# SyncE's planned order kept in the program, and forty warm-up matmuls of other shapes, in an adaLN infini-attention block

## Chip, cores and metric

The kernel runs on one core of one Trainium2 chip. The metric is the device time of one execution in microseconds (us). Engines: PE is TensorE, ACT is ScalarE, DVE is VectorE, POOL is GpSimd, SP is SyncE, which here does nothing but issue DMA transfers.

## The reference

One transformer block over x of 2048 rows and 512 columns: a layer norm modulated by the condition c, causal attention in four segments with a compressive memory carried from segment to segment, a projection, and a feed-forward block with a squared ReLU.

```python
mod = (_silu(c) @ w_mod).reshape(c.shape[0], 6, 1, -1)
sa, ca, ga, sb, cb, gb = (mod[:, 0], mod[:, 1], ...)
h = _layernorm(x, axis=-1) * (1 + ca) + sa
x = x + ga * _A_ref(h, A_wq, A_wk, A_wv, A_wo, A_beta)
h = _layernorm(x, axis=-1) * (1 + cb) + sb
x = x + gb * _B_ref(h, B_w1, B_b1, B_w2, B_b2)
...
# _A_ref: 32 heads of 16, N = 4 segments of L = 512, phi(t) = elu(t) + 1
logits = jnp.einsum("bhqd,bhkd->bhqk", qs, ks) * scale + mask
a_dot = jnp.einsum("bhqk,bhkd->bhqd", _softmax(logits), vs)
o = g * (phi(qs) @ M) / (phi(qs) . z + 1e-6) + (1.0 - g) * a_dot
M = M + jnp.einsum("bhld,bhle->bhde", phi(ks), vs); z = z + phi(ks).sum()
...
# _B_ref: F = 1792
h = x @ w1 + b1
out = jnp.where(h > 0, h, 0) ** 2 @ w2 + b2
```

## The kernel before

**Stages.** The program first makes the modulation rows from c and w_mod (`bmod`, L541) and the normed and transposed rows of the first segment (tiles `lnf`, `HT`), and meanwhile loads the weights. Then come four segments of 512 rows. In each, the 32 heads go in four groups of eight, called units (u = 0 to 15 in all). A unit makes Q and K (`bqk`, L711 to L713) as a sum of three matmuls, since every operand is kept as a rounded half "hi" and a rest "lo". ACT casts the hi half of Q and K into the tile `sg` (L730), DVE subtracts to get the lo half (L732). Twelve small DMAs, the fills (function `fill`, L746 to L754), then rearrange `sg` in SBUF into the wide operand `ST`, from which the logits are formed (`ba`, L799; `bpb`, L956). Of the twelve, four read the hi halves of Q and K, four hi of Q and lo of K, four lo of Q and hi of K. `sg` has one buffer: the next unit's cast waits until the fills of this one have read it. For each quad of heads two more rows, `mt` (L867), go into ST by DMA. ACT makes the exponentials (`pt`), PE multiplies by V (`bpv`), and the outcome goes through DRAM (`o_dram` L1069, read back as `ot` L1117) to the projection with wo (`bwop`, L1101 to L1103). The feed-forward block goes last, over four segments and 14 blocks of F: `bh` (L1262 to L1264), bias `b1c` and ReLU on ACT, square on POOL, DVE or ACT, and `bpf` (L1290 to L1292). Its weights come as raw tiles `wr` (L1228, L1236) and are split in hi and lo (L1230, L1231).

**The order.** Every operation is a node of a planner, the class `Plan` (L226 to L370), with an engine, a duration and a priority. The table `ORDER` (L56 to L213) lists the nodes of each engine, SP among them, in the order in which they are to go; `run` (L1316) lays them out and takes the buffers of the pools, and `emit` writes them in that order. It does so inside `tc.manual_schedule(engines=...)` (L1317), which names the engines for which the order as written is kept. For an engine that isn't named, the framework's scheduler places the instructions itself. Before the change PE, DVE, ACT and POOL are named and SP isn't. On each engine instructions go in order: one that waits for a semaphore holds up all that stand behind it. Each DMA on SP also waits for the one issued eight before it, since eight semaphores go round. A fill, a load of x (L619) or of w_mod (L533) is one DMA; each takes some 0.4 to 0.7 us of SP's time to issue.

**The warm-ups.** PE has nothing to multiply while the first loads come, so 70 matmuls (L510 to L515) of the identity with itself, fp32 128x128, into a PSUM tile that nobody reads, stand in the gaps of the start: 49 ahead of the first `bmod`, 16 more up to the first `bqk`, five later, the last at some 80 us.

Of the kernel before, what the change touches and what calls it, by code (L numbers as in the profile page):

```python
# [9 lines left out]
F32R = mybir.dt.float32r  # L10
BF = mybir.dt.bfloat16
# [6 lines left out]
P = 128  # L18
# [4 lines left out]
F = 1792  # L23
# [202 lines left out]
class Plan:  # L226
# [17 lines left out]
    def op(self, eng, dur, fn, pr, after=(), mode=None, get=(), put=(), nb=0):  # L244
        n = Node()
        n.eng, n.dur, n.fn, n.pr, n.mode, n.get, n.put, n.nb = eng, dur, fn, pr, mode, tuple(get), tuple(put), nb
        n.lat = self.LAT[eng]
        n.outs, n.left, n.seq, n.at = [], 0, len(self.nodes), None
        for a in after:
            if a is not None:  # L250
                a.outs.append(n)
                n.left += 1
        for k in n.put:
            self.users[k] = self.users.get(k, 0) + 1
        self.nodes.append(n)
        return n
# [117 lines left out]
def block_kernel(ctx, tc, x, wq, wk, wv, wo, beta, w1, b1, w2, b2, c, wmod, out):  # L374
    nc = tc.nc
# [22 lines left out]
    ident = const.tile([P, P], F32, name="ident")  # L398
# [15 lines left out]
    sb = ph1.enter_context(tc.tile_pool(name="sb", bufs=1))  # L414
# [29 lines left out]
    PL = Plan(POOLS, ORDER)  # L444
# [3 lines left out]
    def bank(key):  # L448
        if key not in TL:
            TL[key] = ps.tile([P, 512], F32, name=f"b{key[0]}", tag=f"bank{PL.slot[key]}")  # L450
        return TL[key]
# [5 lines left out]
    def buf(pool, key, dt=F32):  # L457
        if key not in TL:
            home = xr_pool if pool == "xr" else sb
            TL[key] = home.tile(SHAPES[pool], dt, name=key[0], tag=f"{pool}{PL.slot[key]}")  # L460
        return TL[key]

    def pe(mode, dur, fn, pr, **kw):
        return op("PE", dur, fn, pr, mode=mode, **kw)

    def act(n, fn, pr, sbuf=False, sc=0, **kw):
        return op("ACT", n / 1200 + (0.095 if sbuf and n > 160 else 0.05) + 0.093 * sc, fn, pr, **kw)
# [4 lines left out]
    def sp(fn, pr, nb, n=1, **kw):  # L472
        return op("SP", 0.65 * n, fn, pr, nb=nb, **kw)
# [17 lines left out]
    def gates():  # L491
# [11 lines left out]
            get=[("#D", ("cs",))], put=["crow"])  # L503
# [4 lines left out]


    wk_ = ("warm",)  # L510
    for i in range(N_WARM):
        pe("F", 0.22, lambda: nc.tensor.matmul(bank(wk_)[:, :P], ident, ident, start=True, stop=True), 50.0,
           get=[("bank", wk_)] if i == 0 else (), put=[wk_], after=[n_w0] if i else ())
        if i == 0:
            n_w0 = PL.nodes[-1]  # L515

# [643 lines left out]
    for s in range(NS):  # L1160
# [6 lines left out]
        for cc in range(4):  # L1167
# [7 lines left out]
            for qd in (0, 1):  # L1175
                i = 2 * u + qd
                a_quad(u, qd, [i + k for k in K_A[qd]], i + K_T[qd])
            if s == 0 and cc == 1:
# [7 lines left out]
                n = pe("F", 0.9, lambda: nc.tensor.matmul(bank(b_), selc.to_broadcast([P, P]), TL[t_], start=True, stop=True),  # L1186
                       m0 + 3.1, after=[MODT[5]], get=[("#D", b_), ("oraw", tkey)], put=[t_])
                n = act(512, lambda: nc.scalar.copy(buf("oraw", tkey), bank(b_)), m0 + 3.11, after=[n], put=[b_])
                sp(lambda: nc.sync.dma_start(gb_dram, TL[tkey][0:1, :]), m0 + 3.12, 1 << 11, after=[n], put=[tkey])
            mem(u, [2 * u + k for k in K_MEM])  # L1190
            for qd in (0, 1):
                i = 2 * u + qd
# [52 lines left out]
    for t in range(4):  # L1245
        wo_tile(4 * NS - 4 + t, z - 2 + 0.3 * t)
    kb = ("b2b",)
    n = sp(lambda: nc.sync.dma_start(buf("xr", kb), bass.AP(tensor=b2.tensor, offset=b2.offset, ap=[[0, P], [1, D]])), z + 0.2, 1 << 18,
           get=[("xr", kb)], after=[X1N[4 * NS - 1]])
# [64 lines left out]
                last = s == NS - 1 and f >= NF - 2  # L1314
                ffn2(s, f, t, z + ST2 * (s * NF + (NF - 1 if last else f) + LAG) + (0.02 * t + 0.001 * f if last else 0.001 * t), RR[s, f])
    PL.run()  # L1316
    with tc.manual_schedule(engines={mybir.EngineType.PE, mybir.EngineType.DVE, mybir.EngineType.Activation, mybir.EngineType.Pool}):  # L1317
        PL.emit()


# [21 lines left out]
```

## Time and profile before

| | before |
|---|---|
| runs | 806.57, 807.46, 807.86 us, median 807.46 |
| span of the profiled execution | 804.3 us |
| PE busy | 792.1 us (98%) |
| DVE, ACT, POOL busy | 537.3, 440.5, 232.9 us |
| DMA moved | 65.23 MB in 51300 packets |
| fills (ST from sg) | 192 of 128 KB |

The profiled execution has no time of its own beside the span; the runs' median is 3.2 us above it. A timeline's row gives start and duration in us, engine (SPq is SyncE's queue of DMA issues), line, operation, tiles out and in, shape, the number of records, and in brackets the engine's idle time before it with what ended it. PE writes two records for one such fp32 matmul of the warm-up.

### The profile page before, as it was taken

To read this page: it belongs to the slowest core of one execution; us is meant where nothing else is said; L and a number is where in the kernel's file an instruction comes from. 1 tells how busy PE (TensorE), PEld (TensorE's weight loads), DVE (VectorE), ACT (ScalarE), POOL (GpSimd) and SP (SyncE) were. 2 spreads that over 40 slices of the span, in tenths; PEclk is the share of its full clock that TensorE was granted. 3 is DMA by queue.
4 is the path that set the end of the run, shared out by engine and by line. 5 is a ranking of instruction groups with operands and counts; after the bars stand their busy time and mean duration, and the time that the engine had idled before them with its cause. 6 is when DMAs were issued, how large, how long until landed. Compare 5 with 4: busy or idle time off the path is not lost.

```text
span 804.3 us, 14894 instructions
## 1 busy us (share of the span) xinstructions
PE 792.1 (98%) x5289; PEld 582.3 (72%) x5289; DVE 537.3 (67%) x1425; ACT 440.5 (55%) x908; POOL 232.9 (29%) x314
## 2 busy tenths in 40 slices
PE   8999999999999999999999999999999999999998
PEld 7876666676666756665766678788888888888886
DVE  4688888779877797777999879864433434424223
ACT  1648866789867896677665744543233323322211
POOL 4555535537655684444332211000000000000000
PEclk9999999999999999999999999999999999999999
DMA  9655562324214442434622143230100010001001
GB/s 309 174 135 123 156 206 71 87 74 107 75 47 106 107 103 54 99 74 99 172 66 80 54 145 105 92 92 13 53 1 0 1 53 0 1 1 53 1 1 52
DMA packets 51300, 65.23 MB, mean 81 GB/s; under 512 B 7829, under 2 KB 24985, under 8 KB 51226
## 3 DMA queue, kind: packets, MB, share of 16 engines
q1 hardware_dynamic: 51074, 64.14, 28.6%
q8 instruction: 42, 0.69, 0.3%
q14 instruction: 32, 0.26, 0.1%
q10 hardware_dynamic: 152, 0.13, 0.1%
HBM read 29.91 MB, written 7.34 MB: 46 GB/s over the span
## 4 chain that ended last, share of the span: by engine, by line
PE 80%; DVE 10%; ACT 4%; DMA 3%; issue 2%; SPq 1%; POOL 1%; DVEq 0%; ACTq 0%; POOLq 0%
PE bpv L1015 7%; PE bpf L1291 6%; PE bpf L1290 6%; PE bpf L1292 6%; PE bh L1264 6%; PE bh L1262 6%; PE bh L1263 6%; PE bpb L956 5%; PE ba L799 5%; PE bqk L711 4%; PE bqk L712 3%; PE bqk L713 3%; DVE ba L804 2%; PE bv L770 2%; PE bwop L1101 2%
## 5 line engine op out<-in xcount | busy, mean ns | idle before, releaser
L804 DVE CUSTOM_DVE_ANT_0 ba<-ba,msk 128x512 f32<-128x512 f32 (+2 forms) x384 | 192.5, 532 | 31.0 <-PE ba L799 23.5
L973 ACT ACTIVATE pt<-bpb 128x512 f32<-128x512 f32 x320 | 171.4, 627 | 30.4 <-PE bpb L956 26.6
L1279 DVE TENSOR_TENSOR r<-r 128x512 f32<-128x512 f32 x56 | 38.7, 691 | 122.2 <-ACT rr L1276 122.1
L1272 ACT ACTIVATE r<-bh,b1c 128x512 f32<-128x512 f32 x56 | 38.5, 687 | 138.6 <-PE bh L1264 97.7
L960 POOL TENSOR_SCALAR_AFFINE_SELECT pt<-pt 128x512 f32<-128x512 f32 x128 | 80.1, 645 | 113.1 <-ACT pt L973 86.7
L1291 PE MATMUL bpf<-W,rr 128*128 128x512 f32 x224 | 88.1, 394 | 0.0
L1290 PE MATMUL bpf<-W,rr 128*128 128x512 f32 x224 | 88.1, 393 | 0.0
L1292 PE MATMUL bpf<-W,rr 128*128 128x512 f32 x224 | 87.6, 391 | 0.0
L1015 PE MATMUL bpv<-pt,VT 128*32 128x512 f32 (+3 forms) x1024 | 80.6, 437 | 0.2 <-DVE mx L804 0.2
L956 PE MATMUL bpb<-ST 64*128 64x256 f32 (+2 forms) x512 | 74.5, 353 | 1.3 <-ACT ac L832 0.4
L799 PE MATMUL ba<-ST 63*128 63x256 f32 (+2 forms) x512 | 73.2, 354 | 1.0 <-DVE mx L804 0.7
L956 PEld LDWEIGHTS bpb<-ST 64*128 64x128 f32 x512 | 46.9, 185 | 27.2 <-issue 6.6
L799 PEld LDWEIGHTS ba<-ST 63*128 63x128 f32 x512 | 44.2, 185 | 30.9 <-issue 10.5
L711 PE MATMUL bqk<-HT,WQK 128*128 128x512 f32 (+1 forms) x136 | 58.7, 431 | 0.2 <-DVE sg L732 0.2
L1276 ACT ACTIVATE rr<-r 128x512 fp32r<-128x512 f32 x56 | 35.4, 632 | 41.2 <-PE bpf L1292 40.1
L804 DVE DVE_READ_ACCUMULATOR2_ANT mx<- 128x1 f32 x384 | 54.1, 141 | 0.1
L712 PE MATMUL bqk<-HT,WQK 128*128 128x512 f32 (+1 forms) x136 | 51.9, 382 | 0.7 <-DVE HT L595 0.7
L713 PE MATMUL bqk<-HT,WQK 128*128 128x512 f32 (+1 forms) x136 | 51.8, 381 | 0.0
L1015 PEld LDWEIGHTS bpv<-pt,VT 128*32 128x32 f32 x1024 | 27.2, 109 | 33.7 <-issue 27.3
L1290 PEld LDWEIGHTS bpf<-W,rr 128*128 128x128 f32 x224 | 42.1, 188 | 9.8
L1291 PEld LDWEIGHTS bpf<-W,rr 128*128 128x128 f32 x224 | 42.0, 188 | 9.6
L1292 PEld LDWEIGHTS bpf<-W,rr 128*128 128x128 f32 x224 | 42.1, 188 | 9.4
(160 smaller groups left out, 1614.1 us busy)
## 6 DMA issues: line engine op xcount, KB each, us to landing
ST<-sg SPq DMA_DIRECT2D x192, 128.0 KB
wr<-in_B_w SPq DMA_DIRECT2D x28, 256.0 KB
xt<-in_A_x SPq DMA_DIRECT2D x16, 256.0 KB
wm<-in_w_mod SPq DMA_DIRECT2D x16, 256.0 KB
xw<-in_A_x SPq DMA_DIRECT2D x16, 256.0 KB
o_dram<-on SPq DMA_DIRECT2D x12, 256.0 KB
ot<-o_dram SPq DMA_DIRECT2D x12, 256.0 KB
out<-X SPq DMA_DIRECT2D x12, 256.0 KB
```

The lines of the kernel that those rows point to most:

```text
L711: nc.tensor.matmul(p[:, c], wh, HT[:, 0, k, c], start=(k == 0), stop=False)
L712: nc.tensor.matmul(p[:, c], wh, HT[:, 1, k, c], start=False, stop=False)
L713: nc.tensor.matmul(p[:, c], wl, HT[:, 0, k, c], start=False, stop=(k == KD - 1))
L799: nc.tensor.matmul(dst[:, c0:c0 + n], ST[b:b + 63, 0, sl, qt * P:(qt + 1) * P], ST[b:b + 63, 1, sl, :n], start=True, stop=True)
L804: nc.vector.tensor_tensor_reduce(i, i, msk[:, 512 - n:], scale=1.0, scalar=-3e38, op0=ALU.add, op1=ALU.max, accum_out=o)
L956: nc.tensor.matmul(dst, ST[b:b + 64, 1, sl, kb * P:(kb + 1) * P], ST[b:b + 64, 0, sl, q0:512], start=True, stop=True)
L960: nc.gpsimd.affine_select(out=ap, in_=ap, pattern=[[0, ap.shape[1]], [1, P]], compare_op=ALU.is_ge, fill=0.0, base=0, channel_multiplier=-1)
L973: ns = [act(512, lambda j=j: nc.scalar.activation(buf("PPP"[n], pt)[:, i + j], bank(keys[j]), AF.Exp, scale=0.25), pr[slot] + 0.01 + 0.001 ...
L1015: nc.tensor.matmul(bank(o)[32 * hq:32 * hq + 32, q0:q0 + src.shape[1]], v[:, a:a + 32], src, start=start, stop=stop, tile_position=(0, 32 ...
L1290: nc.tensor.matmul(p, rh, FF["W2"][:, f, 0], start=(f == 0), stop=False)
L1291: nc.tensor.matmul(p, rh, FF["W2"][:, f, 1], start=False, stop=False)
L1292: nc.tensor.matmul(p, rl, FF["W2"][:, f, 0], start=False, stop=(f == NF - 1))
```

## The change

Two things. First, SP is added to the engines whose written order is kept. Second, of the 70 warm-ups the first 30 stay, and the other 40 come in five groups of eight: with 128 weight columns, with 64, with 32, in bf16, and with 128 weight columns that alternate between two places; all of them stream 512 columns. They read a new tile `wt` (fp32r, 128x512), which one DVE copy of the identity fills at the start, and which holds a buffer of the pool "am" until the last warm-up.

```diff
@@ -508,9 +508,27 @@
     wk_ = ("warm",)
+    wt = sb.tile([P, 512], F32R, name="wt", tag="am0")
+    PL.held["wt"] = [("am", PL.pools["am"].pop(0))]
+    nc.vector.tensor_copy(wt.rearrange("p (a n) -> p a n", a=4), ident[:, None, :].to_broadcast([P, 4, P]))
+    warmed = []
+
+    def warm():
+        p, g = bank(wk_), (len(warmed) - 30) // 8
+        warmed.append(g)
+        if g < 0:
+            nc.tensor.matmul(p[:, :P], ident, ident, start=True, stop=True)
+        elif g == 3:
+            w = wt.bitcast(BF)
+            nc.tensor.matmul(p, w[:, :P], w[:, 512:], start=True, stop=True)
+        else:
+            m = (P, 64, 32, 0, P)[g]
+            a = len(warmed) % 2 * P if g == 4 else 0
+            nc.tensor.matmul(p[:m], wt[:, a:a + m], wt, start=True, stop=True)
+
     for i in range(N_WARM):
-        pe("F", 0.22, lambda: nc.tensor.matmul(bank(wk_)[:, :P], ident, ident, start=True, stop=True), 50.0,
-           get=[("bank", wk_)] if i == 0 else (), put=[wk_], after=[n_w0] if i else ())
+        pe("F", 0.22, warm, 50.0,
+           get=[("bank", wk_)] if i == 0 else (), put=[wk_, "wt"], after=[n_w0] if i else ())
@@ -1314,7 +1332,7 @@
     PL.run()
-    with tc.manual_schedule(engines={mybir.EngineType.PE, mybir.EngineType.DVE, mybir.EngineType.Activation, mybir.EngineType.Pool}):
+    with tc.manual_schedule(engines={mybir.EngineType.PE, mybir.EngineType.DVE, mybir.EngineType.Activation, mybir.EngineType.Pool, mybir.EngineType.SP}):
         PL.emit()
```

ACT and POOL keep the order of their instructions. DVE gains the copy of `wt`, PE's matmuls stand where they stood, with the new shapes in 40 places (19 of them ahead of the first `bmod`, 16 more up to the first `bqk`, five later). The lines behind L512 move by 18; so L748 of before is L766 of after in the rows below.

SP's queue at the start, as the difference of the two programs (w is a raw weight tile of the attention, pad the tile of zeros that clears ST, xt a tile of x rows):

```order
 L505 DMA ge<-in_A_beta 128x32
 L680 DMA w<-in_A_wk 128x4x128
+L680 DMA w<-in_A_wv 128x4x384
 L706 DMA ST<-pad 32x4x512 x6
-L1235 DMA b1c<-in_B_b 128x14x1
-L680 DMA w<-in_A_wv 128x4x384
 L680 DMA w<-in_A_wv 128x4x128
 L637 DMA xt<-in_A_x 128x512 x4
```

The bias load b1c has left the start, and the larger wv load stands ahead of the six clearing DMAs.

SP's queue at the fourth unit of the first segment, before, with the semaphores that each instruction waits for (DMAHW are the eight of the DMAs):

```order
L867 DMA ST_110<-mt_856 1x8x128 [waits DMAHW0_49]
L748 DMA ST_110<-sg_889 32x2x512 [waits DVE_49,DMAHW1_49,PE_49,Activation_49]
L748 DMA ST_110<-sg_889 32x2x512 [waits DMAHW2_49]
L748 DMA ST_110<-sg_889 32x2x512 [waits DMAHW3_49]
L748 DMA ST_110<-sg_889 32x2x512 [waits DMAHW4_49,DVE_49]
L748 DMA ST_110<-sg_889 32x2x512 [waits DMAHW5_49]
L748 DMA ST_110<-sg_889 32x2x512 [waits DMAHW6_49]
L867 DMA ST_110<-mt_1016 1x8x128 [waits DMAHW7_49,Activation_49]
L867 DMA ST_110<-mt_1016 1x8x128 [waits DMAHW0_49]
L748 DMA ST_110<-sg_889 32x2x512 [waits DMAHW1_49,PE_49]
L533 DMA wm_1058<-in_w_mod 128x512 [waits DMAHW2_49,PE_49]
L533 DMA wm_1091<-in_w_mod 128x512 [waits DMAHW3_49,PE_49]
```

The same place after (buffer numbers are two higher):

```order
L885 DMA ST_110<-mt_858 1x8x128 [waits DMAHW7_49]
L766 DMA ST_110<-sg_891 32x2x512 [waits DMAHW0_49,DVE_49]
L766 DMA ST_110<-sg_891 32x2x512 [waits DMAHW1_49,PE_49,Activation_49]
L766 DMA ST_110<-sg_891 32x2x512 [waits DMAHW2_49]
L766 DMA ST_110<-sg_891 32x2x512 [waits DMAHW3_49]
L766 DMA ST_110<-sg_891 32x2x512 [waits DMAHW4_49]
L766 DMA ST_110<-sg_891 32x2x512 [waits DMAHW5_49]
L885 DMA ST_110<-mt_1018 1x8x128 [waits DMAHW6_49,Activation_49]
L885 DMA ST_110<-mt_1018 1x8x128 [waits DMAHW7_49]
L766 DMA ST_110<-sg_891 32x2x512 [waits DMAHW0_49,PE_49]
L551 DMA wm_1060<-in_w_mod 128x512 [waits DMAHW1_49,PE_49]
```

Six fills, two mt rows, a fill and wm loads follow one another as before, but among the six the order is another: before, the wait for DVE's last piece (the lo half of K) stands at the fourth fill, and after, at the first.

SP's queue at the passage from the attention to the feed-forward block, as a difference:

```order
 L1135 DMA ot<-o_dram 128x512
-L1136 DMA xw<-in_A_x 128x512 x3
-L1246 DMA wr<-in_B_w 128x4x128 x2
+L1136 DMA xw<-in_A_x 128x512
+L1246 DMA wr<-in_B_w 128x4x128
+L1136 DMA xw<-in_A_x 128x512
+L1235 DMA b1c<-in_B_b 128x14x1
+L1136 DMA xw<-in_A_x 128x512
+L1246 DMA wr<-in_B_w 128x4x128
 L1136 DMA xw<-in_A_x 128x512 x2
 L1234 DMA gbb<-gb_dram 128x512
```

The first W1 load moves ahead of two xw loads (x rows for the residual sum), and b1c stands between the first and the second W1 load. Elsewhere in SP's queue, the four xt loads of the last segment now stand together behind an o_dram write instead of one by one, and the first wo, ot and xw loads stand together behind fills instead of far ahead of them.

## Prediction

> **What bounds the kernel now.** I began with the page's busy shares and its row of the granted clock.
>
> ```profile
> span 804.3 us, 14894 instructions
> ...
> PE 792.1 (98%) x5289; PEld 582.3 (72%) x5289; DVE 537.3 (67%) x1425; ACT 440.5 (55%) x908; POOL 232.9 (29%) x314
> ...
> PEclk9999999999999999999999999999999999999999
> ```
>
> TensorE (PE) is busy for 792.1 of 804.3 us, and its granted clock is at the top in every slice. No other engine comes near. So a change that leaves the matmuls alone can win only what PE spends waiting. Next comes the view of waits, for PE alone, with total, times and longest in each row.
>
> ```profile
> PE bwarm L512 <- POOL ident masks.py:199: 1.9, 1, 1.9
> PE bmod L541 <- ACT oraw L1039: 1.1, 1, 1.1
> PE bwop L1103 <- DVE oT L1136: 0.9, 1, 0.9
> PE ba L799 <- DVE mx L804: 0.7, 2, 0.4
> PE bqk L712 <- DVE HT L595: 0.7, 2, 0.3
> PE bh L1262 <- ACT lnf L588: 0.5, 1, 0.5
> PE bmod L541 <- DMA wmod<-in_w_mod: 0.4, 1, 0.4
> ```
>
> The first row is the start of the program, before there is anything to multiply; the change can't touch it. The other six add up to 1.1 + 0.9 + 0.7 + 0.7 + 0.5 + 0.4 = 4.3 us. That is about all that a better order of SyncE could win; the price of a worse one has no such cap. The rest of the working goes to the places where SyncE (SP) feeds PE closely.
>
> The span is 804.3 us, and the runs' median is 807.46 (806.57 to 807.86): some 3.2 us lie around the span, and I keep that difference. I call 0.2% (1.6 us) the least that a measurement of this kernel can tell from no change.
>
> **The change part by part: the warm-ups.** The timeline of PE and DVE at the start; columns are start, duration, engine, line, operation, tiles, shape, records (two for each of these matmuls), and the idle time before with its releaser.
>
> ```profile
> 1.90 5.22 PE L512 MATMUL bwarm<-ident 128*128 128x128 f32 x28 [1.90 <-POOL ident masks.py:199]
> ...
> 7.20 8.08 PE L512 MATMUL bwarm<-ident 128*128 128x128 f32 x70
> 15.22 1.06 PE L541 MATMUL bmod<-wmod,cs 128*32 128x512 f32 x8
> 16.21 0.49 PE L512 MATMUL bwarm<-ident 128*128 128x128 f32 x2
> ...
> 18.50 1.06 PE L541 MATMUL bmod<-wmod,cs 128*32 128x512 f32 x6 [0.39 <-DMA wmod<-in_w_mod]
> ...
> 600.76 0.39 PE L1292 MATMUL bpf<-W,rr 128*128 128x512 f32 x1
> 600.99 0.40 PE L1290 MATMUL bpf<-W,rr 128*128 128x512 f32 x1
> ```
>
> ```profile
> 3.01 1.94 DVE L487 TENSOR_SCALAR crow<-crow 4x128 f32<-4x128 f32 x1 [0.38 <-ACT crow L500]
> ```
>
> A warm-up takes 8.08 / 35 = 0.231 us once PE is up to speed (the first fourteen 5.22 / 14 = 0.373). The new ones stream 512 columns. In the FFN a matmul of 512 columns starts 600.99 - 600.76 = 0.23 us after the last one; and four with 32 weight columns take 16.21 - 15.22 = 0.99 us, 0.248 each. So forty exchanges cost between nothing and 40 x (0.248 - 0.231) = 0.7 us, and I take nothing, by the nearest row in form, the FFN's. Nineteen of the forty stand before 15.2 us, ahead of a wait of PE for wmod that ends at 18.50 whatever comes before; the cover is that wait of 0.39 us, against at most 19 x 0.017 = 0.3. About 16 follow up to 26 us. They stand between work for which PE waits on ScalarE and VectorE anyway; if that cover were gone, 16 x 0.017 = 0.3. The last five are at most 0.1. The bf16 form has no row; it streams as many columns, so I give it the same bounds.
>
> The added cast on DVE (128x512, in the row of such a size below 0.70 us) stands ahead of L487. DVE idles 0.38 there, so the constant row `crow` comes up to 0.3 late and with it `bcs`; but warm-ups fill the time up to 15.2. Nothing.
>
> **SyncE at the start.** The bias load `b1c` leaves this place. Timeline of SP, windows of three stretches (length, busy time per engine, granted clock, DMA share, GB/s), and what DVE waits for.
>
> ```profile
> 20.00 1.27 SPq L1217 DMA_DIRECT2D b1c<-in_B_b  x1
> 21.37 2.43 SPq L662 DMA_DIRECT2D w<-in_A_wv  x2
> 23.90 2.66 SPq L619 DMA_DIRECT2D xt<-in_A_x  x4
> ```
>
> ```profile
> 22.00:24.60 2.60, 2.60 (x25) 2.60 (x25) 1.79 (x6) 1.43 (x4) 0.23 (x1) 1.00 0.83 100
> 24.60:31.00 6.40, 5.71 (x45) 5.22 (x44) 4.84 (x10) 6.14 (x14) 1.06 (x1) 1.00 0.92 324
> ```
>
> ```profile
> 30.95 0.70 DVE L569 BATCH_NORM_STATS2 bs<-xt 128x6 f32<-128x512 f32 x1 [0.80 <-DMA xt<-in_A_x]
> ```
>
> It costs 1.27 us of issue, and in the stretch behind it, which I put down to its 1792 single elements, the DMA engines are busy (0.83) but move 100 GB/s instead of 324: 2.6 x (1 - 100/324) = 1.8 us of loads. Without it, wv and the xt loads behind come 1 to 2 us earlier, and DVE's 0.80 goes. PE doesn't wait for that tile: its two waits here are for HT, made of the x tiles that were loaded first. So the gain is between 0 and 0.8; I take 0, since PE's waits list names none.
>
> **SyncE in the unit batches.** Each unit stores twelve ST fills from its tile sg: ScalarE casts the half "hi", VectorE subtracts to get "lo". As the order rows show, the lo half of K, which is ready last, was needed from the fourth fill of a batch on, and now by the first. Timeline at the fourth unit:
>
> ```profile
> 75.16 0.58 ACT L730 CAST sg<-bqk 128x512 fp32r<-128x512 f32 x1
> ...
> 75.77 4.04 SPq L748 DMA_DIRECT2D ST<-sg  x6
> ...
> 76.77 0.69 DVE L732 TENSOR_TENSOR sg<-bqk,sg 128x512 fp32r<-128x512 f32 x1
> ...
> 81.23 1.41 SPq L867 DMA_DIRECT2D ST<-mt  x2
> ...
> 83.51 1.01 SPq L533 DMA_DIRECT2D wm<-in_w_mod  x2
> ...
> 88.09 0.58 ACT L1039 COPY oraw<-bpv 128x512 f32<-128x512 f32 x1
> ...
> 88.76 1.06 PE L541 MATMUL bmod<-wm,cs 128*32 128x512 f32 x8 [1.08 <-ACT oraw L1039]
> ```
>
> SP now starts these six fills after lo, at 76.77 + 0.69 = 77.46 instead of 75.77, and with the same 4.04 us for six they end at about 81.6. The two mt issues stood at 81.23; they move to 81.6, and the fill and the two wm loads (256 KB each) behind them move by the same 0.4. PE needs both wm loads for `bmod` at 88.76. The row names ScalarE's copy; nothing there shows the landing. If the loads land close to the copy, PE loses up to 0.4; if long before, nothing. Five us from issue to use is long, but the fills queue ahead of them. I take 0.4, the upper end, as the 1.08 us wait is the longest of PE's after the start.
>
> A second kind of place: the sg tile has one buffer, so the next unit's cast waits until the twelve fills have landed.
>
> ```profile
> 275.76 1.26 SPq L748 DMA_DIRECT2D ST<-sg  x2
> ...
> 279.91 0.59 ACT L730 CAST sg<-bqk 128x512 fp32r<-128x512 f32 x1
> ...
> 285.32 0.69 DVE L732 TENSOR_TENSOR sg<-bqk,sg 128x512 fp32r<-128x512 f32 x1 [0.79 <-ACT e L737]
> ...
> 371.02 1.07 ACT L730 CAST sg<-bqk 128x512 fp32r<-128x512 f32 x2 [3.31 <-DMA ST<-sg]
> ```
>
> At 279.91 the cast comes 2.9 us after the last fill's issue (275.76 + 1.26 = 277.02); at 371.02 ScalarE waits 3.31 us for such a landing. A later fill passes on to the cast, the subtraction at 285.32 and the next matmul. Where the batch ends no later than before, as when its last six wait for PE to leave their slots, the cost is nothing; where the start's 77.46 - 75.77 = 1.7 us carries through, it is 1.7 at each place. I take 0.3 for all, as the nearest row for what is passed on is the 0.4 above.
>
> **SyncE at the passage to the FFN.** b1c comes back here, between the last xw loads, and the first W1 load moves ahead of them.
>
> ```profile
> 465.06 0.86 SPq L1118 DMA_DIRECT2D xw<-in_A_x  x2
> 466.03 2.61 SPq L1228 DMA_DIRECT2D wr<-in_B_w  x2
> ...
> 470.93 0.50 PE L1103 MATMUL bwop<-WVO,oT 128*128 128x512 f32 x1 [0.86 <-DVE oT L1136]
> ...
> 471.23 0.62 ACT L1230 CAST W<-wr 128x512 fp32r<-128x512 f32 x1 [0.36 <-DMA wr<-in_B_w]
> ...
> 471.99 1.29 DVE L1231 TENSOR_TENSOR W<-wr,W 128x512 fp32r<-128x512 f32 x2
> ```
>
> Here b1c's price is again 1.27 of issue and 1.8 of loads, about 3 us for the second wr, which already makes ScalarE wait 0.36. But its subtraction ends at 471.99 + 1.29 = 473.3, and PE comes to that block only after twelve matmuls of the first, at 472.7 + 12 x 0.23 = 475.5: a reserve of 2.2. So between 0 and 0.8; I take nothing, because the first W1 load, now earlier, takes its place off the queue behind b1c.
>
> **Loads that now go in a body.** The four xt loads of the last segment stand together behind an o_dram write, and the first wo, ot and xw loads, which had been sent far ahead, stand together behind fills. Were one of them late, the longest wait for a transfer that I quote gives its price, 3.3 us (the row at 371.02); below nothing I see no gain, since nothing on PE waits for a load of theirs now. They are loaded early enough for none of them to stand in PE's list, so I take 0.
>
> **Sum.** 0 (warm-ups, cast) + 0 (start) + 0.4 + 0.3 (batches) + 0 (passage) + 0 (loads in a body) = +0.7. On the profiled execution 804.3 + 0.7 = 805.0; with the 3.2 around it **808.2 us**. A span of such a size says: the same.
>
> [...] The first fourteen warm-ups ran at 0.373 against 0.231, while the row of the granted clock shows no step. [...]
>
> **The rivals.**
> Slower, by the fills: the start of a batch that waits for lo pushes its end. It decides from the point where a batch's last fill comes more than the next unit's reserve later; at 371.02 and 279.91 there is next to none. Price: 1.7 us at two or three places, 3 to 5 us, less what PE has queued; I take +3, 810.5. For it: one buffer of sg, sixteen units, and an SP that stands in front of whatever it can't issue, mt rows and weight loads included. Against: half of a batch waits for lo in any case, and PE's list names no fill as a releaser.
> Slower, by a cold PE: 64 and 32 weight columns don't keep PE at its pace, and one more stretch like the first comes before 30 us: 14 x (0.373 - 0.231) = +2.0, with the 0.7: 810.2. For it only those first fourteen; against it that bmod, with 32 columns, follows warm-ups without losing pace.
> Faster: the start keeps 0.8 of DVE's wait, W1 lies ready early, and the waits 0.4 (wmod) and 0.86 (oT) at PE shrink with the queues: -0.8 - 0.4 - 0.86 = -2.1, with nothing lost in the batches: 805.4. Against: the wmod loads stand ahead of all that is moved, and oT is VectorE's own chain.
> No effect: order on paper alone. SP was never the bound and every load has reserve: 807.5. Against: the fills and b1c do move.
>
> **How the numbers follow.** Forecast +0.7 (from -0.8, the start's end alone, up to +1.6, where it would count as slower): 0.45. Fills: 0.27. Cold PE: 0.05. Faster: 0.13. No effect: 0.10. Faster by over 0.2% (below 805.85) takes most of the fourth case, 0.10. Slower by over 0.2% (above 809.07) takes the second but for a twentieth, the third, and a little of the forecast's upper end: 0.35. Within: 0.55. The range reaches from the faster case, 805.4, to 811.4, where the fills' 3 to 5 us are cut: some 0.08 lies above and 0.07 below.
>
> **What would show it.** In the changed profile, SP's first fill of a unit should start after VectorE's subtraction (about 77.5 at the fourth unit) and wm at about 83.9; PE's wait ahead of `bmod` there should be near 1.5. DVE's wait for xt at 31 us should be gone, b1c issued near 466, and ScalarE's wait for wr beside it. Warm-ups should keep 0.23 us each, and the first bqk matmuls (256 columns) their pace of before. I'm wrong if PE's waits grow by more than 1.6 us in all, if a fill turns up as PE's releaser, or if the passage at 470 us holds PE for over 2 us.

## The result, and the profile after

The changed kernel takes 808.62 us (median of 21 runs, 806.72 to 810.19), the kernel before 807.46 (median of 21 beside them, 805.87 to 810.11). The ratio is 1.0013, with a 95% interval of 1.0004 to 1.0022: slower by some 1.05 us. Single executions of either kernel lie up to 4.2 us apart, and the two profiled ones, spans 804.3 and 808.0, differ by more than the medians. The execution profiled after took 809.76 us at its span of 808.0: some 1.8 us lie around a span, and not the 3.2 of the prediction. By that the profiled execution of before was some 1.4 us quicker than the median one (an estimate: 807.46 - 1.8 - 804.3). So below the traces say where time is lost, and the medians and ratios how much.

The page after, its head:

```profile
span 808.0 us, 14803 instructions
...
PE 793.8 (98%) x5248; PEld 580.2 (72%) x5249; DVE 537.5 (67%) x1426; ACT 440.8 (55%) x908; POOL 233.0 (29%) x314
...
PEclk9999999999999999999999999999999999999999
```

PE has 41 matmul and 40 weight-load records fewer than before (5248 and 5249 against 5289 each): an fp32 warm-up is two matmuls and two weight loads, a new one is one of each (98 matmul records for the 49 ahead of the first `bmod` before, 19 for the 19 new ones there). The longest waits of PE after:

```profile
...
PE ba L817 <- DVE mx L822: 1.0, 2, 0.7
PE bwop L1121 <- DVE oT L1154: 1.0, 1, 1.0
...
PE blnq L600 <- ACT phi L757: 0.7, 1, 0.7
PE bv L789 <- POOL WVO L694: 0.5, 1, 0.5
...
PE bqk L731 <- POOL WQK L694: 0.4, 1, 0.4
```

Two waits of before are gone: the 1.1 us of `bmod` at 88.8 us and the 0.4 for wmod. The three largest new ones, for phi, WVO and WQK (0.7 + 0.5 + 0.4 = 1.6), all lie between 32 and 51 us. What is ahead of them, in the timeline of SyncE after:

```profile
12.06 0.38 SPq L680 DMA_DIRECT2D w<-in_A_wk  x1
17.56 0.38 SPq L680 DMA_DIRECT2D w<-in_A_wv  x1
17.98 7.29 SPq L706 DMA_DIRECT2D ST<-pad  x6
25.32 1.39 SPq L680 DMA_DIRECT2D w<-in_A_wv  x1
```

and the same place before:

```profile
12.64 7.32 SPq L688 DMA_DIRECT2D ST<-pad  x6
```

SyncE stands still from 12.4 to 17.6 us. The wv load, which now comes ahead of the six clearing DMAs, goes into a buffer that a load of w_mod had, so it waits until PE has read that: the first `bmod` group ends at 16.35 + 1.06 = 17.41.

```profile
16.35 1.06 PE L559 MATMUL bmod<-wmod,cs 128*32 128x512 f32 x8
```

The clearing DMAs behind it, which wait for nothing of the kind, begin at 17.98 instead of 12.64. In the stretch 16 to 20 us the DMA engines are busy for a share of 0.46, against 1.08 before; the columns are stretch, length, granted clock, DMA share and GB/s. After, then before:

```profile
16.00:20.00 4.00, 1.00 0.46 133
20.00:24.00 4.00, 1.00 1.03 344
```

```profile
16.00:20.00 4.00, 1.00 1.08 337
```

The transfers that should have been done by 20 us run up to 24, and the second wv load comes at 25.32 instead of about 23, though b1c is gone from the queue. That reaches ScalarE and then PE. Timeline of both after:

```profile
30.27 0.62 ACT L690 CAST WVO<-w 128x512 fp32r<-128x512 f32 x1 [1.75 <-DMA w<-in_A_wv]
...
32.83 0.50 PE L731 MATMUL bqk<-HT,WQK 128*128 128x512 f32 x1 [0.41 <-POOL WQK L694]
...
37.88 0.51 PE L789 MATMUL bv<-WVO,HT 128*128 128x512 f32 x1 [0.49 <-POOL WVO L694]
...
48.04 1.07 ACT L748 CAST sg<-bqk 128x512 fp32r<-128x512 f32 x2 [0.92 <-DMA ST<-sg]
...
51.03 0.66 PE L600 MATMUL blnq<-ident,xt 128*128 128x128 f32 x4 [0.66 <-ACT phi L757]
```

ScalarE waits 1.75 us for wv, POOL gets its halves of the weights later, and the fills of the first unit end later, for which the next cast waits 0.92.

### The profile page after: what moved, and what is told of

Read it like the earlier page. It is cut to its first block, busy times and chain, and to the rows that moved or that the text cites. A ratio compares the mean times of both kernels' runs of the same rounds, so it can differ in the third digit from the quotient of the medians.

```text
span 808.0 us, 14803 instructions
## 1 busy us (share of the span) xinstructions
PE 793.8 (98%) x5248; PEld 580.2 (72%) x5249; DVE 537.5 (67%) x1426; ACT 440.8 (55%) x908; POOL 233.0 (29%) x314
## 4 chain that ended last, share of the span: by engine, by line
PE 80%; DVE 10%; ACT 3%; issue 2%; DMA 2%; SPq 2%; POOL 0%; DVEq 0%; ACTq 0%; POOLq 0%
PE bpv L1033 7%; PE bpf L1309 6%; PE bh L1282 6%; PE bpf L1308 6%; PE bpf L1310 6%; PE bh L1280 6%; PE bh L1281 6%; PE ba L817 6%; PE bpb L974 5%; PE bqk L729 3%; DVE ba L822 3%; PE bqk L731 2%; PE bqk L730 2%; PE bwop L1119 2%; PE blnq L600 2%
## 5 line engine op out<-in xcount | busy, mean ns | idle before, releaser
L978 POOL TENSOR_SCALAR_AFFINE_SELECT pt<-pt 128x512 f32<-128x512 f32 x128 | 80.2, 647 | 112.4 <-ACT pt L991 87.4
L1308 PEld LDWEIGHTS bpf<-W,rr 128*128 128x128 f32 x224 | 42.1, 188 | 9.8
L759 POOL TENSOR_SCALAR e<-e 128x512 f32<-128x512 f32 x24 | 35.8, 1490 | 45.7 <-ACT e L755 45.6
L1309 PEld LDWEIGHTS bpf<-W,rr 128*128 128x128 f32 x224 | 42.0, 188 | 9.6
```

What stands on the lines that cost most here:

```text
L978: nc.gpsimd.affine_select(out=ap, in_=ap, pattern=[[0, ap.shape[1]], [1, P]], compare_op=ALU.is_ge, fill=0.0, base=0, channel_multiplier=-1)
L1308: nc.tensor.matmul(p, rh, FF["W2"][:, f, 0], start=(f == 0), stop=False)
L1309: nc.tensor.matmul(p, rh, FF["W2"][:, f, 1], start=False, stop=False)
```

## The experiments

Ratios are against the kernel before, run on the same chip beside each set; its medians there were 807.8 (e1 to e4), 807.71 (e5 to e9) and 807.41 (e10 to e13). The three sets ran on three chips, so runs of different sets are compared by their ratios.

| run | median, us | ratio (95%) |
|---|---|---|
| e1 SyncE alone | 809.95 | 1.0021 (1.0009 to 1.0034) |
| e2 warm-ups alone | 805.29 | 0.9969 (0.9957 to 0.9981) |
| e3 change, wv behind clears | 807.43 | 0.9997 (0.9988 to 1.0006) |
| e4 change, hi fills first | 812.47 | 1.0062 (1.0046 to 1.0078) |
| e5 order of before kept | 810.75 | 1.0037 (1.0023 to 1.0051) |
| e6 e5, fill ahead of mt | 811.07 | 1.0036 (1.0021 to 1.0052) |
| e8 e5 with new warm-ups | 807.70 | 1.0001 (0.9989 to 1.0013) |
| e9 e1, wv behind clears | 808.96 | 1.0011 (0.9996 to 1.0025) |
| e10 fewer PE instructions | 804.58 | 0.9967 (0.9956 to 0.9979) |
| e11 new shapes, old count | 808.30 | 1.0013 (1.0002 to 1.0023) |
| e12 e9, last fill first | 807.72 | 1.0003 (0.9990 to 1.0016) |
| e13 still fewer | 805.44 | 0.9978 (0.9969 to 0.9986) |

### First set: which half, and which step

Three theories. S: the cost is SyncE's wait at the start. F: it is the fills that need the lo half of K first. W: it is the new warm-ups and their copy.

**e1**, SyncE's order kept, old warm-ups:

```diff
-    with tc.manual_schedule(engines={... mybir.EngineType.Pool}):
+    with tc.manual_schedule(engines={... mybir.EngineType.Pool, mybir.EngineType.SP}):
```

Expected:

> SyncE's order kept, the 70 old warm-ups. Theory S (the cost comes from SyncE's queue at the start, where the larger wv load stands ahead of the six clearing DMAs and waits for PE): +1.2 us on the kernel before, as the whole change. Theory F (fills that need the lo half of K first): +1.2 as well. Theory W (the new warm-ups and their DVE copy cost it): 0, within 0.3.

Measured: 1.0021, some 1.7 us slower. SyncE's half is the one that costs, and by its ratio it costs more alone than the whole change does, though the two intervals overlap.

**e2**, the other half: the new `warm` and its copy, with SP left out of the engines.

> The new warm-ups and their copy, SyncE placed by the framework's scheduler as before. Theories S and F: 0, within 0.3, since the copy's delay lies ahead of PE's wait for wmod. Theory W: +1.2.

Measured: 0.9969, 2.5 us **faster** than before. No theory expected that. W is wrong in sign, and S and F lack a term that is larger than the whole result.

**e3**, one step of SyncE's order taken back (node 149 is the larger wv load, 158 to 160 are the clearing DMAs):

```diff
-... 5 138 149 158-160 148 ...
+... 5 138 158-160 149 148 ...
```

> The whole change, with one step back in SyncE's queue: the larger wv load behind the six clearing DMAs. Theory S: the six clearing DMAs are issued from about 12.6 instead of 18.0, PE's waits for WQK, WVO and phi between 32 and 51 us go, and the time falls by 1 us or more on the changed kernel, to 807.5 or below. Theories F and W: no change on the changed kernel, +1.2 on the one before.

Measured: 0.9997; against the change's 1.0013 that is 0.16%, 1.3 us less; the two intervals just touch (up to 1.0006 here, from 1.0004 there). Of the new waits those for WQK and WVO are gone, and 0.3 is left of the one for phi. S holds for this step.

**e4**, in each half batch of six fills those that need the lo half of K come last (the fourth unit's first half):

```diff
-... 620 624 623 619 622 621 ...
+... 624 619 622 621 620 623 ...
```

> The whole change, but within each half batch of six fills those that need the lo half of K come last again. Theory F: -0.7 or more on the changed kernel, 807.9 or below. Theory S: -0.4 at most, and only at the fourth unit.

Measured: 1.0062, 3.9 us slower than the change. Its timeline, SyncE and ScalarE, then PE, and last ScalarE's same cast in the change, shows where that time goes:

```profile
362.60 5.23 SPq L766 DMA_DIRECT2D ST<-sg  x4
...
377.22 1.07 ACT L748 CAST sg<-bqk 128x512 fp32r<-128x512 f32 x2 [5.51 <-DMA ST<-sg]
```

```profile
379.03 0.65 PE L974 MATMUL bpb<-ST 64*128 64x512 f32 x2 [2.17 <-ACT VT L795]
```

```profile
374.07 1.07 ACT L748 CAST sg<-bqk 128x512 fp32r<-128x512 f32 x2 [2.77 <-DMA ST<-sg]
```

This is the tight place at 371 us of the prediction. My exchange brought a fill forward here whose slot in ST PE was still reading: four fills take SyncE 5.23 us instead of 4 x 0.65, ScalarE's wait for the last one grows from 2.77 in the change (3.31 before) to 5.51, and PE waits 2.17 behind it. So a fill in the wrong place costs what the rival said, but the run is a poor test of F. What it tells of F it tells before that place: the same `bpv` matmul that starts at 333.32 us in the trace of before starts at 336.94 in the change's and at 337.37 in e4's, so that no gain is to be seen.

### Second set: where the warm-ups' gain comes from

In e2 the scheduler had also put one fill ahead of the two mt rows at the fourth unit. Theory Q: that pair is the gain. Theory W+: the warm-ups are. To hold the queue fixed, I wrote the order that the scheduler had made for the kernel before into the table.

**e5**, old warm-ups, that order kept. The bias load must be free to go early, and some loads (two xt, two wo, one ot and one xw) can't go where the scheduler had them, since the planner has no buffer for them by then:

```diff
-    n_b1 = sp(..., z - 2.8, 1 << 14, after=[N_FFN])
+    n_b1 = sp(..., z - 2.8, 1 << 14)
...
-... 5 138 149 158-160 148 ...
+... 5 138 158-160 2629 149 148 ...
...
```

> Old warm-ups, SyncE's order kept, but the order written is the one that the scheduler had made for the kernel before (with b1c early, wv behind the clearing DMAs, fills as before; only five loads that lie far from any use stay where the plan has them). All theories: as the kernel before, 807.5 within 0.5. If it is slower by 1 us or more, keeping an order costs something of itself.

Measured: 1.0037, 3 us slower. As a copy of before it failed: the wo, ot and xw loads ended amid a unit's fills, and ScalarE and PE wait there as in e4 (SyncE and ScalarE, then PE).

```profile
363.36 0.59 SPq L1091 DMA_DIRECT2D wo<-in_A_wo  x1
...
374.12 1.07 ACT L730 CAST sg<-bqk 128x512 fp32r<-128x512 f32 x2 [5.30 <-DMA ST<-sg]
```

```profile
375.93 0.65 PE L956 MATMUL bpb<-ST 64*128 64x512 f32 x2 [1.97 <-ACT VT L777]
```

So whether keeping an order costs something of itself it doesn't answer. As a base for e6 and e8, which share the flaw, it serves.

**e6**, e5 with the pair exchanged:

```diff
-... 621 371 627 ...
+... 621 627 371 ...
```

> As the last one, with one pair exchanged: at the fourth unit the seventh fill goes ahead of the two mt rows, as the scheduler had put it in the run of the warm-ups alone. Theory Q (the gain of the warm-ups alone, 2.5 us, comes from this pair): 805.0 to 805.5. Theory W+ (it comes from the warm-ups): 807.5, within 0.5.

Measured: 1.0036, as e5. Q falls.

**e8**, e5 with the new warm-ups.

> New warm-ups with the same kept order of before. Theory W+: 805.0 to 806. Theory Q: 807.5, within 0.5.

Measured: 1.0001, 2.9 us below e5, on the same order of SyncE. So the warm-ups gain by themselves; the level of 805 to 806 that I expected was missed, for which the flaw in the base, 3 us, is the likely reason.

**e9**, e1 with node 149 behind the clearing DMAs, as in e3.

> Old warm-ups, the planned order of SyncE, with the larger wv load behind the clearing DMAs. With the run of SyncE alone (1.7 to 2.1 us slower than before) it isolates that step: theory S expects 1 us or more off, 808.7 or below. If wv's place matters only beside the new warm-ups: 809.5 or above.

Measured: 808.96, 1.0011; e1 was 1.0021. The medians differ by 1.0 us in the sense of S, but the intervals overlap, and it fell 0.3 short of what I had asked for.

### Third set: why other warm-ups gain

The traces of before and e1 show what runs with the old warm-ups share. A packet of queue q8, "instruction", begins in both between 15.4 and 16.8 us and another between 85.9 and 87.4. In the kernel before they begin at 15.5 and 86.0, each while a load for a `bmod` is under way: PE waits 0.39 us for wmod ahead of 18.50, and the wm loads, issued from 83.51 on, are for the `bmod` at 88.76. The view of DMA queues in two windows before (packets, MB, share of 16 engines):

```profile
q1 hardware_dynamic: 544, 0.48, 101.9%
q8 instruction: 1, 0.02, 5.0%
```

```profile
q1 hardware_dynamic: 196, 0.34, 87.3%
q8 instruction: 1, 0.02, 5.6%
```

The windows are 15.4 to 16.8 and 85.9 to 87.1 us. One packet of 16 KB takes 5.0% of 16 engines in 1.4 us: 0.050 x 16 x 1.4 = 1.1 us. On which of the engines it lay, and by what way it makes a load late, isn't shown. The page counts 42 such packets, 0.69 MB, for 2 x 5289 records of PE, some 250 to a packet. So I took them for PE's own instruction fetches, whose times would then depend on how many instructions PE has had; no view names their engine. Whether they cost PE time is what these runs test. Theory I: the new warm-ups are 80 PE instructions fewer, so every fetch comes later, past those two loads. Theory C: the shapes themselves help.

**e10**, the kernel before with 20 of the 40 warm-ups doubled in width and 20 left out, so fp32 and the same time, but 80 instructions fewer:

```diff
+        elif j % 2 == 0:
+            nc.tensor.matmul(bank(wk_)[:, :2 * P]..., ident, ident[:, None, :].to_broadcast([P, 2, P]), start=True, stop=True)
```

> The kernel before, SyncE placed by the scheduler; of the 40 warm-ups that the change gives other shapes, 20 stream 256 columns of the identity in fp32 and 20 are left out: the same time on PE in the old form, but 80 PE instructions fewer, as many fewer as in the change. No copy on DVE. Theory I (the new warm-ups gain because PE's 16 KB instruction fetches, queue q8, fall elsewhere against the loads of wmod and wm): 805.3 within 0.7, and no wait of 1 us for wm at 88 us. Theory C (the shapes themselves help, PE's pace or clock): 807.5 within 0.7.

Measured: 804.58, 0.9967. The whole gain of e2 without a new shape. In the window 15.4 to 16.8 there is no q8 packet; PE's second `bmod` group doesn't wait, and the one at 87 us waits 0.32, for ScalarE:

```profile
q1 hardware_dynamic: 677, 0.48, 110.4%
```

```profile
17.45 1.06 PE L551 MATMUL bmod<-wmod,cs 128*32 128x512 f32 x8
...
87.31 1.06 PE L551 MATMUL bmod<-wm,cs 128*32 128x512 f32 x8 [0.32 <-ACT HT L605]
```

**e11**, the reverse: e2 with each new warm-up cut in two halves of 256 columns, so as many instructions as before.

```diff
-            nc.tensor.matmul(p[:m], wt[:, a:a + m], wt, start=True, stop=True)
+            for h in (0, 256):
+                nc.tensor.matmul(p[:m, h:h + 256], wt[:, a:a + m], wt[:, h:h + 256], start=True, stop=True)
```

> The new warm-ups alone, each cut in two matmuls of 256 columns, so that PE has as many instructions as before the change; SyncE placed by the scheduler. Theory I: the gain of the warm-ups alone (2.5 us) goes, 807.5 within 0.7, the first fetch is at 15 to 16 us and the wait for wm at 88 us is back. Theory C: 805.3 within 0.7.

Measured: 808.30, 1.0013. The gain is gone, and q8 is back in the window 15.4 to 16.8, as are both waits:

```profile
q1 hardware_dynamic: 630, 0.48, 106.8%
q8 instruction: 1, 0.02, 5.0%
```

```profile
18.27 1.06 PE L561 MATMUL bmod<-wmod,cs 128*32 128x512 f32 x6 [0.40 <-DMA wmod<-in_w_mod]
...
89.05 1.06 PE L561 MATMUL bmod<-wm,cs 128*32 128x512 f32 x8 [1.57 <-ACT pt L993]
```

With the same shapes as e2 it is 3.5 us slower by the ratios, and with the old shape e10 is as fast as e2: C falls. PE's list of waits has a third one here, 0.8 us for a wm load.

**e13**, e10 with 10 warm-ups of 512 columns and 30 left out, 120 instructions fewer (`j % 4 == 0`).

> As the run with 20 wider warm-ups, but with 10 that stream 512 columns and 30 left out: 120 PE instructions fewer than before. Theory I: the fetches move on by half as much again, past the loads at 17 and 88 us; 805 to 806, though another load may now meet one. Theory C: 807.5.

Measured: 805.44, 0.9978, within what I expected, and not better than e10. No q8 packet begins from 15.2 to 18.6 us or from 85.3 to 88.7, and neither the second `bmod` group (17.79) nor the one at 87.70 waits.

In this set SyncE was left to the scheduler, and its order was not the same throughout: e10 and e13 have e2's fill ahead of the two mt rows, e11 has the order of before. By their times alone Q would fit these runs as well as I. The second set separates the two at the load itself. e6 has that pair and the old warm-ups, e8 the order of before and the new ones; the `bmod` of the fourth unit in e6, then in e8:

```profile
89.26 1.06 PE L541 MATMUL bmod<-wm,cs 128*32 128x512 f32 x8 [1.33 <-DMA wm<-in_w_mod]
```

```profile
87.65 1.06 PE L559 MATMUL bmod<-wm,cs 128*32 128x512 f32 x8 [0.38 <-DMA wm<-in_w_mod]
```

The wait stays with the pair exchanged and shrinks with the count, so I holds. The other traces agree: in six with the old count (before, e1, e5, e6, e9, e11) PE waits 0.9 to 1.8 us for this `bmod`; in the seven with a smaller count it waits 0 to 0.4. In before, e1 and e11 a q8 packet begins between 85.9 and 87.4 us, in the change, e2, e10 and e13 none does. So at this load a fetch isn't free: PE's wait beside it is 0.9 to 1.6 us (e1, before, e11). At the earlier load the old count costs a wait of 0.4 in before, e5, e9 and e11, though not in e1; of the smaller count the change, e2, e3, e4, e10 and e13 have none. The traces place only part of the gain, though: at this `bmod` e10 is 88.76 - 87.31 = 1.45 us ahead of the kernel before, and the medians differ by 2.8. Where the rest lies isn't shown; the profiled execution of before was a quick one.

**e12**, e9 with one exchange more. In the kept order the last fill of a unit at 277 us goes behind the o_dram write, which before it preceded (1666 is the fill, 1318 the write):

```diff
-... 1670 1318 1666 ...
+... 1670 1666 1318 ...
```

> Old warm-ups, SyncE's order kept, wv behind the clearing DMAs, and one more exchange: the last fill of the unit at 277 us goes ahead of the o_dram write, as in the kernel before. If that fill holds up the next cast: 1 to 1.5 us off the run without the exchange (809.0), so 807.5 to 808.0, and PE's wait of 1.5 us for phi at 283 us goes. If the batch's start is what counts: 809.0 within 0.5.

Measured: 807.72, 1.0003; e9 had 1.0011. By the ratios that is 0.6 us off (1.2 by the medians, but on two chips), with overlapping intervals, so less than was expected of the fill is shown. The wait at 283 to 285 us is gone. What it looked like in e1, SyncE and ScalarE, then PE:

```profile
277.17 0.42 SPq L1069 DMA_DIRECT2D o_dram<-on  x1
277.63 0.61 SPq L748 DMA_DIRECT2D ST<-sg  x1
...
282.71 0.58 ACT L730 CAST sg<-bqk 128x512 fp32r<-128x512 f32 x1 [2.14 <-DMA ST<-sg]
```

```profile
285.26 0.50 PE L799 MATMUL ba<-ST 63*128 63x256 f32 x3 [1.54 <-ACT phi L739]
```

The cast comes 5 us after the fill's issue, and PE loses 1.5. In e12 the same cast:

```profile
280.07 0.59 ACT L730 CAST sg<-bqk 128x512 fp32r<-128x512 f32 x1
```

With wv and that fill put back, what SyncE's kept order still costs can't be told from nothing. The fastest measured are e10 and e2, equal within their intervals; e10 is the kernel before, with SyncE left to the scheduler and 80 PE instructions fewer in the warm-up, 0.33% under before.

## Why the prediction was right, and where its steps were not

The time was forecast at 808.2 and came out at 808.62, "the same" by the bound of 0.2%. But that is luck: two terms of opposite sign were missing, +1.3 (SyncE at the start, by e3) and -2.5 (the warm-ups alone, by e2). Nor do these two make up the measured +1.05; what is open is said at the end.

- **Warm-ups, 0.** Failed. Their pace was as said (nineteen new ones in 16.35 - 11.80 = 4.55 us, 0.239 each), and no second stretch at the pace of the first fourteen came; what makes those slower no run shows. But I priced only their time. With fewer instructions the q8 packets come later (15.5 and 86.0 us before, 16.9 and 91.4 in the change), past two loads: -2.5 us by e2, part of which the traces place.

```profile
11.80 4.62 PE L527 MATMUL bwarm<-wt 128*128 128x512 f32 x19
```

- **The cast, under 0.70 and hidden.** Right in effect, and in size only sometimes. In the change's trace it takes 2.60 us, in e2's 0.57, as said. It doesn't reach PE: the change's list of PE's waits names neither the copy nor `crow`, and in e2 and e11, which have the copy, the first `bmod` starts at 15.09 and 15.05 us, and before, without it, at 15.22. The change, then e2:

```profile
2.56 2.60 DVE L513 CAST wt<-ident 128x512 fp32r<-128x512 f32 x1
5.08 0.30 DVE L487 TENSOR_SCALAR crow<-crow 4x128 f32<-4x128 f32 x1
```

```profile
2.56 0.57 DVE L513 CAST wt<-ident 128x512 fp32r<-128x512 f32 x1
```

- **SyncE at the start, 0 (a gain of up to 0.8).** Failed, in sign. I looked at what b1c's absence frees and at the rows moved, and didn't price the wait of the moved load: wv needs PE to be done with a buffer, and six clearing DMAs stood behind it. 1.3 us by e3. DVE's wait for xt, which was to go, grew from 0.80 to 2.75:

```profile
34.37 0.70 DVE L587 BATCH_NORM_STATS2 bs<-xt 128x6 f32<-128x512 f32 x1 [2.75 <-DMA xt<-in_A_x]
```

- **The fourth unit, +0.4.** Failed at its last step, PE's wait. The queue moved as worked out: the change's trace is 51.03 - 48.88 = 2.15 us late by here (the `blnq` above), and less that its six fills begin at 77.46 and wm at 83.90. But PE has no wait at all there, which by e6 and e8 I put down to the fetch: the q8 packet that had begun amid the wm loads, at 86.0 us, now begins behind them, at 91.4. The `blnq` before, and the change's queue and `bmod`:

```profile
48.88 0.66 PE L582 MATMUL blnq<-ident,xt 128*128 128x128 f32 x4
```

```profile
79.61 4.06 SPq L766 DMA_DIRECT2D ST<-sg  x6
83.77 1.41 SPq L885 DMA_DIRECT2D ST<-mt  x2
...
86.05 1.11 SPq L551 DMA_DIRECT2D wm<-in_w_mod  x2
```

```profile
89.76 1.07 PE L559 MATMUL bmod<-wm,cs 128*32 128x512 f32 x8
```

The wm loads, issued 2.5 us later than before, are in time for a `bmod` 1.0 later. Before, my doubt about the row's releaser was justified (in e1, e5, e6 and e9 the row names the wm load), but my answer wasn't: it wasn't a matter of when SyncE issued.

- **The tight fills, +0.3.** That a late fill is passed on to the cast and to PE was right, and so was the place (280 us): with the old warm-ups PE waits 1.5 us in e1, and putting the fill back gains 0.6 by the ratios of e9 and e12; in the change's own trace PE waits 0.3 for phi there. The cause was another: what delays the fill is the o_dram write ahead of it, not lo coming first, for which e4 shows nothing.
- **The passage, 0.** Right. b1c was issued at 468.66 in 0.43 us, ScalarE's wait for wr grew from 0.36 to 1.21, and PE's wait there went from 0.86 to 0.99:

```profile
468.66 0.43 SPq L1235 DMA_DIRECT2D b1c<-in_B_b  x1
...
474.29 0.50 PE L1121 MATMUL bwop<-WVO,oT 128*128 128x512 f32 x1 [0.99 <-DVE oT L1154]
...
475.21 0.62 ACT L1248 CAST W<-wr 128x512 fp32r<-128x512 f32 x1 [1.21 <-DMA wr<-in_B_w]
```

- **Rivals.** "Slower by the fills" needed a fill in a worse place, which e4 gave (+3.9 on the change). "Faster" came only with the warm-ups alone (e2, -2.5), and by a means that I hadn't named. "A cold PE" didn't show.

What stays open: e1 and e2 multiply to 0.9990, the change has 1.0013, some 1.9 us more. The warm-ups gain 0.31 to 0.36% on the scheduler's order and on e5's, and less on the planned order of the change (0.08% from e1, 0.14% from e9 to e3). The wait for wm goes there too (0.89 in e1, none in the change); but PE waits 1.6 for WQK, WVO and phi in the change's trace and 0.3, for WVO, in e1's. Why a faster start loses so much there no run separates.

## What to carry to other kernels

When a queue's order is changed, go through the waits of each moved instruction and name what is queued behind it; here one load that waited for a buffer held up six that waited for nothing. Count an edit's instructions and not only its time: 80 PE instructions fewer were worth 0.31 to 0.36% here (e2, e10, e8 against e5), and with them went some 1 us of PE's wait at one `bmod` (1.08 before and none in e2, 1.33 in e6 and 0.38 in e8). To tell such a phase effect from one of the work itself, change the count at the same work, and the work at the same count, as e10 and e11 do, and hold the order of every queue meanwhile: the scheduler moved a fill along with the count there, and two runs with a kept order were needed to tell them apart.

## What the runs showed of the hardware that was not expected

- What I take for a fetch of PE's instructions is one 16 KB packet of queue q8, 1.1 us long at 15.5 us before (5.0% of 16 engines in 1.4 us). When it comes follows PE's count of instructions: the first of the warm-up begins at 15.5 us before, between 16.8 and 18.6 with 80 instructions fewer (e10), and with 120 fewer none begins from 15.2 to 18.6 (e13). Taking 80 out of the warm-up gained 2.5 and 2.8 us in 807 (e2 and e10 against before), and putting 80 back at the same work lost 3.5 by the ratios (e11 against e2).
- The DVE copy of 128x512 that starts at 2.56 us took 2.60 us in the change and 0.57 in e2. In the change POOL fills the tile VT meanwhile, five fills that take 2.60 us from 2.29 on. Before, with the same five in 2.59, L487 on DVE took 1.94 us at this place; in the change, behind them at 5.08, it takes 0.30. What ties these times together no run shows.
- The DMA of b1c, 1792 single elements, cost SyncE 1.27 us of issue in the crowded start and 0.43 at 468.66.
